# One fused kernel on one core: two tiles turned by TensorE, the last pair's products in another order, and two, not three, second-weight pieces converted in attention

## The chip, the cores and the metric

The kernel runs on one core of a Trainium2 chip. The metric is the device time of one execution in microseconds, as the median of several runs. TensorE multiplies, VectorE (DVE) and ScalarE (ACT) do everything elementwise, GpSimd (POOL) and SyncE (SP) here only issue DMAs.

## What is computed

```python
scores = q @ k.T / sqrt(64) - log(448)           # 4 batches, 12 heads, 448 tokens, 64 wide
x = sigmoid(scores) @ v                          # laid out as 1792 tokens x 768
h = maximum(maximum(x @ w1, x @ w2), x @ w3)     # 768 x 768 each
x = h @ w_out                                    # 768 x 768
h = x @ w_in                                     # 768 x 1024
solu = h * softmax(h)
ln = (solu - mean(solu)) / sqrt(var(solu) + 1e-6) * g_ln
out = ln @ w_out2                                # 1024 x 768
```

Data are float32; the weights arrive as float64 words, which the kernel turns into float32 itself. A matmul runs on numbers split in a high and a low part (hi, lo), as three matmuls: hi by hi, hi by lo, lo by hi.

## The kernel before

**Attention** (span 0 to 203 us) goes over 24 pairs of heads. A visit of a pair has four score products (L253, L257), four sigmoids on ScalarE (L262, L265), and eight matmuls with v (L278) for this pair and the one before. `prep_qk` splits k and q on VectorE, `take_x` copies the result out of PSUM. k, q and v come by SP's queue, v into two buffers in turn. Between pair 12 and the rest, W = w_out @ w_in is formed (`gen_w`, L469), so that later h @ W replaces two layers. Weights come by POOL's queue into five raw buffers (`load_next`, L147); a buffer is loaded again when its weight is done with.

**Background work.** Converting weights is written as generators, and a visit of the second half takes ten steps from them. `convert_w2` converts one piece of w_out2 in 14 steps (two scalings, a multiplication by g, differences, four hi/lo splits on ScalarE and DVE), and SP writes four results to DRAM (L431) through two staging buffers. SECOND says how many of the 16 pieces go beside attention, mixed with the splits of T (12 tiles, two steps each, each one DVE instruction) and the conversion of the first weight group (`convert_group`). LATE says how many go into each of the nine groups of the next stage, RATE how many steps are taken for each matmul there.

**The three 768 x 768 layers** (203 to 434 us): `product` (L604) runs seven products for eight (Strassen-Winograd) in 18 units, with the maximum taken by `sums`. At the end `load_h` fetches h back (hld, L654) and `load_wf` W in two halves of three loads (wf0, wf1; L702). POOL then loads the converted w_out2 from DRAM (w2t, L904).

**Layer 2, SoLU, layer norm and the last layer** (434 us to the end) go over 14 tiles of 128 tokens, in the order 7 to 13, 0 to 6. `layer2` (L682) has 36 matmuls for a tile, into one of two PSUM places; `solu_ln` normalises it on DVE and ScalarE; `split_h` splits the h of the tile after next. Then a tile must be turned. `turn` does it with a DVE transpose of 32 x 32 blocks, a write to DRAM and four reads (L800 to L803); `transposes` with eight transposes on TensorE (L811) and two copies on ScalarE. `plain` names the tiles that take the second way. Two turned tiles are a pair; `operand` splits one of seven operands (A11, A12, S2, S1, S3, S4, A22) into hi and lo with a cast on ScalarE and a subtraction on DVE; `output` runs the seven products P1 to P7 (L864), twelve matmuls each, into four banks x, v, z, w. The names are held in

```python
PROD = {"P1": ("A11", "B11"), "P2": ("A12", "B21"), "P3": ("S4", "B22"), "P4": ("A22", "T4"),
        "P5": ("S1", "T1"), "P6": ("S2", "T2"), "P7": ("S3", "T3")}
```

The first pair's products come after the fourth tile's `layer2`.

**What sets the order.** TensorE's instructions stand in the order of the program everywhere. Up to the end of the three layers that is so for DVE and ScalarE too; in the last part a scheduler orders them, and SP's issues. Each engine, and each queue, goes strictly by its order.

Of the kernel before, what the change touches and what calls it, by code (L numbers as in the profile page):

```python
# [16 lines left out]
P = 128  # L17
# [13 lines left out]
QU, OU = 192, 96  # L31
NG = 3 * FC // 2
RAWS = 5
EARLY, SECOND = 4, 3
LATE = (0, 1, 1, 1, 1, 1, 1, 1, 2)
RING = 10
RATE = (0.46,) + 7 * (0.38,) + (0.4,)
BLOCKS = (3, 0, 1, 2)
WARM = 8
PROD = {"P1": ("A11", "B11"), "P2": ("A12", "B21"), "P3": ("S4", "B22"), "P4": ("A22", "T4"),  # L40
# [5 lines left out]
def sigmoid_attention_max_moe_solu_ln(tc, q, k, v, w123, wo, wi, w2, g, out):  # L46
# [177 lines left out]
    def load_v(pr):  # L224
        if pr >= NP:
            return
        vr = apool.tile([P, 2, 4, D], F32, tag="vr", name=f"vr{pr}", bufs=2)
        sp.dma_start(out=vr, in_=v[pr])
        v_ops[pr] = vr

# [15 lines left out]
    def scores(pr, c):  # L246
        qt, kt = qk_ops[pr]
        sc = ps_sc.tile([P, 2, 512], F32, tag="sc", name=f"sc{pr}_{c}")
        terms = ((0, 0), (1, 0), (0, 1))
        for t, (x, y) in enumerate(terms):  # L250
            start, stop = t == 0, t == len(terms) - 1
            if c == 3:
                pe.matmul(sc[:, 0, :S], lhsT=kt[:, x, c * P :], rhs=qt[:, y], start=start, stop=stop)  # L253
                continue
            for j in range(2):
                rows = slice(j * D, (j + 1) * D)
                pe.matmul(  # L257
                    sc[:, j, :S], lhsT=kt[rows, x, c * P : (c + 1) * P], rhs=qt[rows, y], start=start, stop=stop
                )
        if c == 3:  # L260
            sf = apool.tile([P, S], F32, tag="s3", name=f"sf{pr}_{c}", bufs=2)
            act.activation(sf, sc[:, 0, :S], AF.Sigmoid, bias=bias_s, scale=1.0 / math.sqrt(D))  # L262
        else:
            sf = apool.tile([P, 2, S], F32, tag="sf", name=f"sf{pr}_{c}", bufs=5)
            act.activation(sf, sc[:, :, :S], AF.Sigmoid, bias=bias_s, scale=1.0 / math.sqrt(D))  # L265
        weights[(pr, c)] = sf
# [3 lines left out]
    def attend(pr, n):  # L270
        vr = v_ops[pr]
        c = BLOCKS[n]
        if n == 0:
            pas[pr] = ps_av.tile([P, 512], F32, tag="av", name=f"av{pr}")
        pa = pas[pr]
        sf = weights.pop((pr, c))
        for j in range(2):
            pe.matmul(  # L278
                pa[j * D : (j + 1) * D, :S],
                lhsT=vr[:, j, c],  # L280
                rhs=sf if c == 3 else sf[:, j],
                start=(n == 0),
                stop=(n == 3),
            )
        if n == 3:
            v_ops.pop(pr)
            load_v(pr + 2)

    def take_x(pr):
        pa = pas.pop(pr)[:, :S]  # L290
# [92 lines left out]
    for pr in range(2):  # L383
        load_v(pr)
    prep_qk(0)
    sp.dma_start(out=g_sb, in_=g)
    MID = NP // 2
    for pr in range(MID):
# [49 lines left out]
            return stp.tile([P, 2 * QU], F32, tag="stg", name=name, bufs=2)  # L438
        return state["home"](k, name)

    def mix(first, second, lead=0):
        gens, n = deque([first, second]), 0
        while gens:
            try:
                next(gens[0])
            except StopIteration:
                gens.popleft()
                continue
            yield
            n += 1  # L450
            if n > lead:
                gens.rotate(1)

    pws = {}

# [101 lines left out]
            yield  # L557

    tsplits = [split_t(0, nm, i) for nm in ("T1", "T4", "T3", "T2") for i in range(3)]
    bg.append(mix(run_steps(tsplits + [convert_group(0)]), run_steps(convert_w2(key) for key in w2_second)))  # L560


    attend_rest(MID, 0)
# [91 lines left out]
        hls[t] = hl  # L655

    h2s, lns, uts, lts, hsp = {}, {}, {}, {}, {}
    plain = (tiles[-1],)

    def split_h(t):  # L660
        hh = hsplit.tile([P, FC, P], F32R, tag="hh", name=f"hh{t}")
# [10 lines left out]
                copy(act, hh[:, 4 + f, cols], src)  # L672
                rest(dve, hl[:, 4 + f, cols], src, hh[:, 4 + f, cols])

    def layer2(t, steps):
        if t not in h2s:
            m = tiles.index(t) % 2
            h2s[t] = (ps_h3 if m else ps_h2).tile([P, 2, 512], F32, tag="h2", name=f"h2_{t}")
        hh, hl = hsp[t]
        for n, f in steps:  # L680
            for i, (l, r) in enumerate(((0, 0), (0, 1), (1, 0))):
                pe.matmul(  # L682
                    h2s[t][:, n],
                    lhsT=(hh, hl)[l][:, f],
                    rhs=wfs[f // 3][:, f % 3, r, n * 512 : (n + 1) * 512],
                    start=(f == 0 and i == 0),
                    stop=(f == FC - 1 and i == 2),
                )

    units = [(gi, bp if gi < NG - 1 else 1 - bp) for gi in range(NG) for bp in range(2)]  # L690
    bg.extend(split_t(1, nm, i) for nm, i in FIN)
# [111 lines left out]
            sp.dma_start(out=ut[r * 32 : (r + 1) * 32], in_=u_d[t][:, :, r].rearrange("i f e -> f i e"))  # L803
        uts[t] = ut.rearrange("p i (k t) -> p k i t", k=K2)

    def transposes(t):
        u = lns.pop(t)
        ps = ps_h2.tile([P, 2, 512], F32, tag="h2", name=f"pt{t}").rearrange("p a (k t) -> p (a k) t", k=4)
        ut = tp.tile([P, K2, P], F32, tag="ut", name=f"ut{t}", bufs=3)
        for kc in range(K2):  # L810
            pe.transpose(ps[:, kc], u[:, kc * P : (kc + 1) * P], ident)  # L811
        for n in range(2):
            copy(act, ut[:, 4 * n : 4 * n + 4], ps[:, 4 * n : 4 * n + 4])
        uts[t] = ut.rearrange("p k (i t) -> p k i t", i=4)

    ops, parts = {}, {}

    def part(p, nm):
        t = uts[tiles[2 * p + int(nm[1]) - 1]]
# [14 lines left out]
    def more_operands(p):  # L834
        a11, a12, a21, a22 = (part(p, nm) for nm in ("A11", "A12", "A21", "A22"))
        s1 = tp.tile([P, 4, P], F32, tag="s1", name=f"s1_{p}", bufs=1).rearrange("p k (i t) -> p k i t", i=4)
        tt(s1, a21, a22, ALU.add)
        tt(a21, a11, a21, ALU.subtract)
        tt(a11, s1, a11, ALU.subtract)
        parts.update({(p, "S1"): s1, (p, "S3"): a21, (p, "S2"): a11, (p, "S4"): a12})  # L840
        for nm in ("S2", "S1", "S3"):
            operand(p, nm)
        tt(a12, a12, a11, ALU.subtract)

# [5 lines left out]
        t = f_tile(nm, i, name) if nm != "e" else ew.tile([P, S], F32, tag="e", name=name, bufs=3)  # L850
        return t[:, :HU]

    def output(p, between=None):
        places = "xvzw" if p < TT // 2 - 1 else "zvxw"
        bank = {nm: ps_o.tile([P, 512], F32, tag=at, name=f"o{nm}{p}")[:, :HU] for nm, at in zip("xvzw", places)}

        def prod(b, name, start, stop):
            a, bn = PROD[name]
            op = ops.pop((p, a))
            wt, off, w = next((w2t[n], OU * nms.index(bn), OU * len(nms)) for n, nms in enumerate(PIECES) if bn in nms)  # L860
            for kc in range(4):
                for i, (l, r) in enumerate(((0, 0), (0, 1), (1, 0))):
                    c0 = off + r * w
                    pe.matmul(  # L864
                        bank[b],
                        lhsT=op[:, l, kc],
                        rhs=wt[:, kc, :, c0 : c0 + OU],
                        start=(start and kc == 0 and i == 0),
                        stop=(stop and kc == 3 and i == 2),
                        skip_group_check=True,  # L870
                    )

        def put(i, j, t, cols=slice(0, HU), eng=sp):
            r = tiles[2 * p + i]
            eng.dma_start(out=out[r * P : (r + 1) * P, j * HU : (j + 1) * HU][:, cols], in_=t[:, cols])

        e1, u2, u3, c21 = (block(f"{nm}{p}") for nm in ("e1", "u2", "u3", "cx"))
        prod("x", "P1", True, False)
        act.copy(e1, bank["x"])
        prod("z", "P2", True, True)  # L880
        tt(e1, bank["z"], e1, ALU.add)
        put(0, 0, e1)
        operand(p, "S4")
        operand(p, "A22")
        prod("x", "P6", False, False)
        act.copy(u2, bank["x"])
        prod("v", "P5", True, True)
        tt(u2, bank["v"], u2, ALU.add)
        prod("x", "P7", False, False)
        act.copy(u3, bank["x"])  # L890
        tt(u3, bank["v"], u3, ALU.add)
        put(1, 1, u3)
        prod("w", "P3", True, True)
        tt(u2, bank["w"], u2, ALU.add)
        put(0, 1, u2)
        if between:
            between()
        prod("x", "P4", False, True)
        act.copy(c21, bank["x"])
        put(1, 0, c21)  # L900

    for n in (3, 0, 2, 1):
        for kc in range(4):
            pool.dma_start(out=w2t[n][:, kc].bitcast(F32), in_=w2_d[n][kc])  # L904
    for n, t in enumerate(tiles):
        if n < 2:
            layer2(t, first_f[0 if n else 2 :])
        else:
            layer2(t, [(m, f) for m in range(2) for f in range(FC)])
        solu_ln(t)  # L910
        if t not in plain:
            turn(t)
        if n + 3 < TT:
            load_h(tiles[n + 3])
        if n + 2 < TT:
            split_h(tiles[n + 2])
        if n >= 2 and n % 2 == 0:
            first_operands(n // 2 - 1)
            more_operands(n // 2 - 1)
        elif n >= 3:  # L920
            p = n // 2 - 1
            output(p, (lambda: transposes(tiles[-1])) if n == TT - 1 else None)
    first_operands(TT // 2 - 1)
    more_operands(TT // 2 - 1)
    output(TT // 2 - 1)

    for cm, _ in reversed(p3):
        shut(cm)
# [55 lines left out]
```

## Time and profile before

| what | us |
|---|---|
| three runs: lowest, median, highest | 681.09, 682.87, 684.08 |
| the profiled execution | 678.11 |
| its span, first to last instruction | 676.3 |
| busy: TensorE, DVE, ScalarE | 653.4, 486.6, 316.9 |
| two successive visits of attention begin | 150.68, 156.66 |

The profiled execution is one run of its own, somewhat under the three timed ones; 1.8 us of it lie outside the span. Times in the rows below are counted from the start of the span.

### The profile page before, as it was taken

The page shows a single profiled execution, that of the slowest core. Times are in us where ns is not written, and L with a number is a line of the kernel's source. Part 1 is how long each engine was busy: PE and PEld are TensorE (multiplying, and loading weights), DVE is VectorE, ACT ScalarE, POOL GpSimd, SP SyncE. Part 2 cuts the span into 40 slices and gives each one's busy share as a digit, 9 for nine tenths or more (in the row PEclk, how much of TensorE's full clock was granted, in tenths as well). Part 3 has the DMA queues.
Part 4 walks back from the last instruction along what each step waited for, and adds up shares of the span by engine and source line. Part 5 has one row for each costly group of instructions (what it writes and reads, how often), then busy time and mean ns, then how long its engine had stood idle before and what let it go on. Part 6 is the DMA issues. An engine that isn't in the chain of part 4 may idle for free.

```text
span 676.3 us, 9636 instructions
## 1 busy us (share of the span) xinstructions
PE 653.4 (97%) x3354; PEld 535.4 (79%) x3354; DVE 486.6 (72%) x1052; ACT 316.9 (47%) x639; POOL 53.4 (8%) x103
## 2 busy tenths in 40 slices
PE   9999999999999999999999999995699999999997
PEld 6555588644449999999999999884599898989887
DVE  4799987687768678757777576483849495958573
ACT  5888534688776544444434433231424242324142
POOL 1111111000010110110110100220000000000000
PEclk9999999999999999999999999998799999999999
DMA  8688679955540333531453415999433333233131
GB/s 270 216 259 251 197 243 342 312 162 187 163 162 1 125 110 121 201 119 64 141 175 109 120 64 155 400 404 356 129 100 90 113 104 115 75 98 120 53 110 47
DMA packets 55441, 111.27 MB, mean 165 GB/s; under 512 B 6112, under 2 KB 36832, under 8 KB 54624
## 3 DMA queue, kind: packets, MB, share of 16 engines
q1 hardware_dynamic: 46800, 67.95, 30.7%
q0 software_dynamic: 8448, 42.47, 19.0%
q8 instruction: 26, 0.43, 0.2%
q10 hardware_dynamic: 144, 0.23, 0.1%
q14 instruction: 23, 0.19, 0.1%
HBM read 77.34 MB, written 33.29 MB: 164 GB/s over the span
## 4 chain that ended last, share of the span: by engine, by line
PE 76%; DVE 10%; DMA 7%; ACT 4%; issue 3%; SPq 0%; ACTq 0%; DVEq 0%
PE x L604 19%; PE h L682 13%; PE v L604 10%; PE ox L864 9%; PE av L278 7%; PE z L604 5%; PE sc L257 4%; DMA u_d<-ub 2%; PE ov L864 2%; PE ow L864 2%; PE oz L864 2%; DMA w_d<-ws 2%; PE sc L253 2%; ACT sf L265 1%; DMA ut<-u_d 1%
## 5 line engine op out<-in xcount | busy, mean ns | idle before, releaser
L682 PE MATMUL h<-wf,hh 128*128 128x512 f32 x336 | 103.5, 389 | 0.0
L278 PE MATMUL av<-sf,vr 128*64 128x448 f32 x384 | 77.7, 546 | 0.4 <-DMA vr<-in_v 0.4
L682 PEld LDWEIGHTS h<-wf,hh 128*128 128x128 f32 x336 | 63.0, 188 | 12.8
L265 ACT ACTIVATE sf<-sc,bias_s 128x896 f32<-128x896 f32 x72 | 68.1, 1011 | 2.7 <-PE sc L257 2.4
L682 PE MATMUL h<-wf,hl 128*128 128x512 f32 x168 | 65.4, 389 | 0.0
L278 PEld LDWEIGHTS av<-sf,vr 128*64 128x64 f32 x384 | 25.4, 136 | 41.5 <-issue 35.9
L257 PE MATMUL sc<-qt,kt 64*128 64x448 f32 x432 | 51.7, 376 | 2.3 <-ACT sf L262 2.2
L644 ACT COPY u<-x 128x448 f32<-128x448 f32 x36 | 19.2, 532 | 68.3 <-PE x L604 68.3
L147 POOL DMA_DIRECT2D raw<-in_w x52 | 28.4, 545 | 274.8 <-DVE w2s L57 122.9
L469 PE MATMUL pw<-wi_t,r_wo 128*128 128x512 f32 x216 | 49.6, 390 | 0.0
L257 PEld LDWEIGHTS sc<-qt,kt 64*128 64x128 f32 x432 | 38.5, 184 | 13.6 <-issue 4.8
L469 PEld LDWEIGHTS pw<-wi_t,r_wo 128*128 128x128 f32 x216 | 40.4, 188 | 9.4 <-issue 1.0
L864 PE MATMUL ox<-w2t,opA 128*128 128x384 f32 x168 | 34.5, 355 | 10.4 <-ACT opA L52 10.3
L864 PEld LDWEIGHTS ox<-w2t,opA 128*128 128x128 f32 x168 | 31.2, 198 | 12.1 <-ACT opA L52 11.1
L771 DVE TENSOR_REDUCE st<-h 128x1 f32<-128x1024 f32 x14 | 17.0, 1214 | 32.2 <-PE h L682 32.2
L864 PE MATMUL ox<-w2t,opS 128*128 128x384 f32 x168 | 33.7, 351 | 5.2 <-ACT opS L52 5.2
L682 PEld LDWEIGHTS h<-wf,hl 128*128 128x128 f32 x168 | 31.5, 188 | 6.5
L864 PEld LDWEIGHTS ox<-w2t,opS 128*128 128x128 f32 x168 | 31.1, 196 | 5.8 <-ACT opS L52 5.6
L604 PE MATMUL x<-T3h,S 128*128 128x448 f32 x108 | 33.7, 366 | 0.0
L604 PE MATMUL x<-B11h,A 128*128 128x448 f32 x108 | 33.7, 366 | 0.0
L604 PE MATMUL x<-T2h,S 128*128 128x448 f32 x108 | 33.6, 365 | 0.0
L604 PE MATMUL v<-B22h,S 128*128 128x448 f32 x108 | 33.6, 365 | 0.0
(152 smaller groups left out, 1388.9 us busy)
## 6 DMA issues: line engine op xcount, KB each, us to landing
raw<-in_w POOLq DMA_DIRECT2D x52, 384.0 KB, 3.9
w_d<-w2s SPq DMA_DIRECT2D x48, 192.0 KB, 2.0
w2t<-w_d POOLq DMA_DIRECT2D x12, 768.0 KB, 14.6
u_d<-ub SPq DMA_DIRECT2D x13, 512.0 KB, 3.0
ut<-u_d SPq DMA_DIRECT2D x52, 128.0 KB, 3.1
kr<-in_k SPq DMA_DIRECT2D x24, 256.0 KB, 3.5
vr<-in_v SPq DMA_DIRECT2D x24, 256.0 KB, 3.9
raw<-in_wi POOLq DMA_DIRECT2D x16, 384.0 KB, 4.5
```

The lines of the kernel that those rows point to most:

```text
L147: pool.dma_start(out=t, in_=source(key).rearrange("p (n t) -> p n t", t=2))
L253: pe.matmul(sc[:, 0, :S], lhsT=kt[:, x, c * P :], rhs=qt[:, y], start=start, stop=stop)
L257: pe.matmul(sc[:, j, :S], lhsT=kt[rows, x, c * P : (c + 1) * P], rhs=qt[rows, y], start=start, stop=stop)
L265: act.activation(sf, sc[:, :, :S], AF.Sigmoid, bias=bias_s, scale=1.0 / math.sqrt(D))
L278: pe.matmul(pa[j * D : (j + 1) * D, :S], lhsT=vr[:, j, c], rhs=sf if c == 3 else sf[:, j], start=(n == 0), stop=(n == 3),)
L469: pe.matmul(ps, lhsT=wt[:, a, cols], rhs=wi_t[:, b, c0 : c0 + 512], start=(i == 0), stop=(i == 3 * KC - 1))
L604: pe.matmul(ps, lhsT=l, rhs=r, start=(start and c == 0 and i == 0), stop=(stop and c == 2 and i == 2), skip_group_check=True)
L644: act.copy(e, ps)
L682: pe.matmul(h2s[t][:, n], lhsT=(hh, hl)[l][:, f], rhs=wfs[f // 3][:, f % 3, r, n * 512 : (n + 1) * 512], start=(f == 0 and i == 0), stop=( ...
L771: dve.tensor_reduce(out=nmax, in_=ps, axis=AX.XY, op=ALU.max, negate=True)
L864: pe.matmul(bank[b], lhsT=op[:, l, kc], rhs=wt[:, kc, :, c0 : c0 + OU], start=(start and kc == 0 and i == 0), stop=(stop and kc == 3 and i ...
```

## The change

Four things change. (1) `plain` takes the first two tiles of layer 2 too: they are turned on TensorE, into the four banks of the output products, each behind the first half of the layer of the tile two places on. (2) In the last pair P4 gets a bank of its own and runs third, its operand A22 is split earlier and S3 later, and the operands A11 and A12 are made before the last tile is turned. (3) SECOND is 2 in place of 3, LATE ends with 3 pieces in place of 2, the last RATE is 0.52, and `mix` takes two steps of the first work for one of the second beside attention. (4) v has three buffers, and the sigmoid's small tile one.

```diff
-EARLY, SECOND = 4, 3
-LATE = (0, 1, 1, 1, 1, 1, 1, 1, 2)
+EARLY, SECOND = 4, 2
+LATE = (0, 1, 1, 1, 1, 1, 1, 1, 3)
 RING = 10
-RATE = (0.46,) + 7 * (0.38,) + (0.4,)
+RATE = (0.46,) + 7 * (0.38,) + (0.52,)
...
-        vr = apool.tile([P, 2, 4, D], F32, tag="vr", name=f"vr{pr}", bufs=2)
+        vr = apool.tile([P, 2, 4, D], F32, tag="vr", name=f"vr{pr}", bufs=3)
...
-            sf = apool.tile([P, S], F32, tag="s3", name=f"sf{pr}_{c}", bufs=2)
+            sf = apool.tile([P, S], F32, tag="s3", name=f"sf{pr}_{c}", bufs=1)
...
-            load_v(pr + 2)
+            load_v(pr + 3)
...
     prep_qk(0)
+    load_v(2)
...
-    def mix(first, second, lead=0):
-        gens, n = deque([first, second]), 0
+    def mix(first, second, lead=0, share=1):
+
+        gens, n = [first, second], 0
         while gens:
...
+            at = n >= lead and (n - lead) % (share + 1) == share
             n += 1
-            if n > lead:
-                gens.rotate(1)
+            gen = gens[min(at, len(gens) - 1)]
+            if next(gen, "end") == "end":
+                gens.remove(gen)
+            else:
+                yield
...
-    bg.append(mix(run_steps(tsplits + [convert_group(0)]), run_steps(convert_w2(key) for key in w2_second)))
+    bg.append(mix(run_steps(tsplits + [convert_group(0)]), run_steps(convert_w2(key) for key in w2_second), 0, 2))
...
-    plain = (tiles[-1],)
+    plain = (tiles[0], tiles[1], tiles[-1])
...
+            if (n, f) == (0, FC - 1) and between:
+                between()
...
+        for n, ps in enumerate(banks):
+            for i in range(4):
+                kc = 4 * n + i
+                pe.transpose(ps[:, i * P : (i + 1) * P], u[:, kc * P : (kc + 1) * P], ident)
+        for n, ps in enumerate(banks):
+            copy(act, ut[:, 4 * n : 4 * n + 4], ps.rearrange("p (k t) -> p k t", k=4))
...
+    def turn_first(i):
+        transposes(tiles[i], [ps_o.tile([P, 512], F32, tag="xvzw"[2 * i + m], name=f"pt{i}_{m}") for m in range(2)])
...
-        operand(p, "S4")
-        operand(p, "A22")
+        operand(p, "S3" if p == LAST else "S4")
+        operand(p, "S4" if p == LAST else "A22")
+        if p == LAST:
+            bank["y"] = ps_h3.tile([P, 2, 512], F32, tag="h2", name="oy")[:, 0, :HU]
+            prod("y", "P4", True, True)
         prod("x", "P6", False, False)
...
+        if p == LAST:
+            tt(c21, bank["y"], u3, ALU.add)
+            put(1, 0, c21)
...
+        if p == LAST - 1:
+            first_operands(LAST)
+            turn_last()
         prod("x", "P4", False, True)
...
         else:
-            layer2(t, [(m, f) for m in range(2) for f in range(FC)])
...
+            layer2(t, steps, (lambda: turn_first(n - 2)) if n < 4 else None)
+        if n == 2:
+            finish(1)
+            first_operands(0)
+        elif n == 3:
+            more_operands(0)
+        if n != 1:
+            finish(n)
```

`finish` is `solu_ln` and, for a tile that isn't in `plain`, `turn`.

The first place is ScalarE at the first output pair (tiles 7 and 8; u10 is the exponential of the fourth tile, hh12 the high half of h for the sixth tile, e10 the copy of P1). Before:

```order
L52 CAST opA11_0_4776<-ut7_4607 128x512
L52 CAST opA12_0_4779<-ut7_4607 128x512
L780 ACTIVATE st9_4739<-st9_4739 128x1
L781 ACTIVATE st9_4739<-st9_4739 128x1
L52 CAST hh12_4862<-hld12_4766 128x512
L52 CAST hh12_4862<-hs0_3_2670 128x128
L52 CAST hh12_4862<-hs1_3_2617 128x128
L879 COPY e10_4874<-ox0_4870 128x384
L772 ACTIVATE u10_4836,st10_4833<-h2_10_4796,st10_4833 128x1024
L52 CAST opS2_0_4786<-ut7_4607 128x512
```

and now:

```order
L52 CAST hh12_4874<-hld12_4771 128x512
L52 CAST hh12_4874<-hs0_3_2644 128x128
L52 CAST hh12_4874<-hs1_3_2591 128x128
L774 ACTIVATE u10_4848,st10_4845<-h2_10_4781,st10_4845 128x1024
L890 COPY e10_4886<-ox0_4882 128x384
L52 COPY ut8_4802<-pt1_0_4800 128x512
L52 COPY ut8_4802<-pt1_1_4801 128x512
L52 CAST opS2_0_4835<-ut7_4689 128x512
L52 CAST opS1_0_4838<-s1_0_4831 128x512
L52 CAST opS3_0_4841<-ut8_4802 128x512
```

The casts of A11 and A12 have moved far ahead, in among the work on tile 8. Two copies of the second turned tile (ut8) are new, and stand behind hh12, u10 and e10; the cast of S2 follows them.

The second place is SP's queue at the end of the three layers (w2s are converted pieces on their way to DRAM, hld tiles of h, wf0 and wf1 the halves of W). Before:

```order
L431 DMA w2_d0_99<-w2s3_3_0_4326 128x384
L431 DMA w2_d1_100<-w2s3_3_1_4335 128x384
L431 DMA w2_d2_101<-w2s3_3_2_4344 128x384
L654 DMA hld7_4358<-h_d_103 128x4x128
L654 DMA hld8_4360<-h_d_103 128x4x128
L654 DMA hld9_4362<-h_d_103 128x4x128
L702 DMA wf0_4367<-w_d_98 128x2048 x3
L431 DMA w2_d3_102<-w2s3_3_3_4373 128x192
L702 DMA wf1_4413<-w_d_98 128x2048 x3
```

and now:

```order
L654 DMA hld7_4344<-h_d_103 128x4x128
L654 DMA hld8_4346<-h_d_103 128x4x128
L654 DMA hld9_4348<-h_d_103 128x4x128
L704 DMA wf0_4353<-w_d_98 128x2048 x3
L432 DMA w2_d0_99<-w2s3_3_0_4362 128x384
L432 DMA w2_d1_100<-w2s3_3_1_4370 128x384
L432 DMA w2_d2_101<-w2s3_3_2_4380 128x384
L432 DMA w2_d3_102<-w2s3_3_3_4388 128x192
L704 DMA wf1_4413<-w_d_98 128x2048 x3
```

Three of the four writes of the last piece have moved from ahead of hld7 to between wf0 and wf1.

The third place is TensorE's end, from the transposes of the last tile on (ox, ov, oz, ow, oy are banks, op the operands of pair 5 and, last, 6). Before:

```order
L811 MATMUL pt6_6331<-ident_4420,un6_6233 128x128 x8
L864 MATMUL ox5_6235<-w2t2_4538,opA22_5_6273 128x384 x12
L864 MATMUL ox6_6377<-w2t3_4539,opA11_6_6357 128x384 x12
L864 MATMUL oz6_6379<-w2t0_4536,opA12_6_6360 128x384 x12
L864 MATMUL ox6_6377<-w2t2_4538,opS2_6_6367 128x384 x12
L864 MATMUL ov6_6378<-w2t1_4537,opS1_6_6370 128x384 x12
L864 MATMUL ox6_6377<-w2t1_4537,opS3_6_6373 128x384 x12
L864 MATMUL ow6_6380<-w2t0_4536,opS4_6_6412 128x384 x12
L864 MATMUL ox6_6377<-w2t2_4538,opA22_6_6415 128x384 x12
```

and now:

```order
L814 MATMUL pt_last_6349<-ident_4420,un6_6245 128x128 x8
L875 MATMUL ox5_6247<-w2t2_4538,opA22_5_6285 128x384 x12
L875 MATMUL ox6_6389<-w2t3_4539,opA11_6_6343 128x384 x12
L875 MATMUL oz6_6391<-w2t0_4536,opA12_6_6346 128x384 x12
L875 MATMUL oy_6430<-w2t2_4538,opA22_6_6375 128x384 x12
L875 MATMUL ox6_6389<-w2t2_4538,opS2_6_6382 128x384 x12
L875 MATMUL ov6_6390<-w2t1_4537,opS1_6_6385 128x384 x12
L875 MATMUL ox6_6389<-w2t1_4537,opS3_6_6424 128x384 x12
L875 MATMUL ow6_6392<-w2t0_4536,opS4_6_6427 128x384 x12
```

P4 of the last pair (opA22_6) has moved from the end to the third place, into bank oy.

## Rows read from the trace of the kernel before

**Rows 1.** The page, part 1: busy time of each engine
```profile
PE 653.4 (97%) x3354; PEld 535.4 (79%) x3354; DVE 486.6 (72%) x1052; ACT 316.9 (47%) x639; POOL 53.4 (8%) x103
```

**Rows 2.** Waits on TensorE, whole span: us in total, times, longest
```profile
PE ox L864 <- ACT opA L52: 10.3, 2, 9.2
PE ox L864 <- ACT opS L52: 5.2, 1, 5.2
PE sc L257 <- ACT sf L262: 2.2, 4, 1.0
...
PE av L278 <- DMA vr<-in_v: 0.4, 1, 0.4
```

**Rows 3.** Chain that ended last, 434 to 516 us: start, us, what
```profile
434.15 6.87 PE h L682 x30
...
441.04 1.24 DVE st L771
...
443.54 1.23 DVE u L773
...
449.83 15.94 DMA u_d<-ub
...
467.11 6.83 DMA ut<-u_d
...
474.04 0.63 ACT opA L52
...
485.27 0.60 DVE ut L60
...
485.89 0.63 ACT opS L52
...
486.56 3.78 PE ox L864 x12
490.34 2.16 PE ov L864 x12
...
498.90 16.32 PE h L682 x72
```

**Rows 4.** Stretches: us, busy time of each engine, PEclk, DMA share, GB/s
```profile
140.00:160.00 20.00, 19.59 (x125) 10.24 (x123) 18.23 (x46) 17.20 (x30) 0.76 (x1) 1.00 0.52 168
425.00:430.00 5.00, 5.00 (x26) 4.53 (x25) 1.41 (x5) 2.29 (x6) 0.00 (x0) 1.00 1.02 421
470.00:475.00 5.00, 0.29 (x1) 0.29 (x2) 2.41 (x6) 0.96 (x2) 0.00 (x0) 0.50 0.79 214
485.00:490.00 5.00, 3.44 (x11) 3.22 (x12) 5.00 (x14) 3.11 (x7) 0.00 (x0) 0.66 0.32 92
```

**Rows 5.** Chain that ended last, 640 to 677 us
```profile
653.17 0.89 PE pt L811 x8
...
657.26 0.70 DVE opA L57
...
658.00 2.03 PE ox L864 x10
```

**Rows 6.** ScalarE in order of time, 652 to 658 us
```profile
654.10 1.08 ACT L52 COPY ut<-pt 128x512 f32<-128x512 f32 x2 [2.56 <-PE pt L811]
```

**Rows 7.** Loads of w2t (L904): ns; first and last issue; landing
```profile
L904 POOL DMA_DIRECT2D w2t<-w_d x16: 530/530/562, 434.6 to 454.9; - x16
...
DMA to landing us min/median/max: 5.9/12.5/17.1
```

**Rows 8.** DMA issued 422.82 to 423.5 us: x, KB each, us to landing
```profile
wf<-w_d SPq DMA_DIRECT2D x1, 1024.0 KB, 16.4
```

**Rows 9.** TensorE in order of time, 439 to 440 us
```profile
439.46 0.62 PE L682 MATMUL h<-wf,hh 128*128 128x512 f32 x2
```

**Rows 10.** DMA issued 439 to 443 us
```profile
hld<-h_d SPq DMA_DIRECT2D x1, 256.0 KB, 19.8
```

**Rows 11.** DMA issued 125 to 204 us
```profile
raw<-in_w POOLq DMA_DIRECT2D x8, 384.0 KB, 4.3
```

More of the change, by code (lines that the diff above doesn't have):

```diff
@@ L439, in staging @@
         return state["home"](k, name)
-    def mix(first, second, lead=0):
-        gens, n = deque([first, second]), 0
+    def mix(first, second, lead=0, share=1):
+        gens, n = [first, second], 0
         while gens:
[L444 to L449, printed above, removed]
-            n += 1
-            if n > lead:
-                gens.rotate(1)
+            at = n >= lead and (n - lead) % (share + 1) == share
+            n += 1
+            gen = gens[min(at, len(gens) - 1)]
[3 more added lines that the diff above has]
+                yield
     pws = {}
@@ L673, in split_h, with layer2 @@
                 rest(dve, hl[:, 4 + f, cols], src, hh[:, 4 + f, cols])
-    def layer2(t, steps):
+    def layer2(t, steps, between=None):
         if t not in h2s:
@@ L804, in turn, with transposes, turn_last @@
         uts[t] = ut.rearrange("p i (k t) -> p k i t", k=K2)
-    def transposes(t):
+    def transposes(t, banks):
         u = lns.pop(t)
-        ps = ps_h2.tile([P, 2, 512], F32, tag="h2", name=f"pt{t}").rearrange("p a (k t) -> p (a k) t", k=4)
         ut = tp.tile([P, K2, P], F32, tag="ut", name=f"ut{t}", bufs=3)
[L810 to L813, printed above, removed]
-        uts[t] = ut.rearrange("p k (i t) -> p k i t", i=4)
+        for n, ps in enumerate(banks):
[4 more added lines that the diff above has]
+            copy(act, ut[:, 4 * n : 4 * n + 4], ps.rearrange("p (k t) -> p k t", k=4))
+        uts[t] = ut.rearrange("p k (i t) -> p k i t", i=4)
+    def turn_first(i):
+        transposes(tiles[i], [ps_o.tile([P, 512], F32, tag="xvzw"[2 * i + m], name=f"pt{i}_{m}") for m in range(2)])
+    def turn_last():
+        ps = ps_h2.tile([P, 2, 512], F32, tag="h2", name="pt_last")
+        transposes(tiles[-1], [ps[:, m] for m in range(2)])
     ops, parts = {}, {}
+    LAST = TT // 2 - 1
     def part(p, nm):
@@ L840, in more_operands @@
         parts.update({(p, "S1"): s1, (p, "S3"): a21, (p, "S2"): a11, (p, "S4"): a12})
-        for nm in ("S2", "S1", "S3"):
+        for nm in ("S2", "S1") if p == LAST else ("S2", "S1", "S3"):
             operand(p, nm)
@@ L851, in block, with output @@
         return t[:, :HU]
-    def output(p, between=None):
-        places = "xvzw" if p < TT // 2 - 1 else "zvxw"
+    def output(p):
+        places = "xvzw" if p < LAST else "zvxw"
         bank = {nm: ps_o.tile([P, 512], F32, tag=at, name=f"o{nm}{p}")[:, :HU] for nm, at in zip("xvzw", places)}
@@ L888, in output @@
         tt(u2, bank["v"], u2, ALU.add)
-        prod("x", "P7", False, False)
+        prod("x", "P7", False, p == LAST)
         act.copy(u3, bank["x"])
+        if p == LAST:
+            tt(c21, bank["y"], u3, ALU.add)
+            put(1, 0, c21)
         tt(u3, bank["v"], u3, ALU.add)
@@ L895, in output @@
         put(0, 1, u2)
-        if between:
-            between()
+        if p == LAST:
+            return
+        if p == LAST - 1:
+            first_operands(LAST)
+            turn_last()
         prod("x", "P4", False, True)
@@ L904, in sigmoid_attention_max_moe_solu_ln, with finish @@
             pool.dma_start(out=w2t[n][:, kc].bitcast(F32), in_=w2_d[n][kc])
+    def finish(n):
+        solu_ln(tiles[n])
+        if tiles[n] not in plain:
+            turn(tiles[n])
     for n, t in enumerate(tiles):
+        steps = [(m, f) for m in range(2) for f in range(FC)]
         if n < 2:
@@ L908, in sigmoid_attention_max_moe_solu_ln @@
         else:
-            layer2(t, [(m, f) for m in range(2) for f in range(FC)])
-        solu_ln(t)
-        if t not in plain:
-            turn(t)
+            layer2(t, steps, (lambda: turn_first(n - 2)) if n < 4 else None)
[6 more added lines that the diff above has]
+            finish(n)
         if n + 3 < TT:
@@ L916, in sigmoid_attention_max_moe_solu_ln @@
             split_h(tiles[n + 2])
-        if n >= 2 and n % 2 == 0:
+        if n >= 4 and n % 2 == 0:
             first_operands(n // 2 - 1)
@@ L920, in sigmoid_attention_max_moe_solu_ln @@
         elif n >= 3:
[L921 to L925, printed above, removed]
+            output(n // 2 - 1)
+    operand(LAST, "A22")
+    more_operands(LAST)
+    output(LAST)
     for cm, _ in reversed(p3):
```

## The prediction, made before the changed kernel was run

> **What bounds the kernel now.** I read the page's busy times first: TensorE is busy 653.4 us, 97% of the span [rows 1]. The reader sees there that no other engine is near, and that all that can be won without taking matmuls away is the 23 us in which TensorE stands still, plus what those pauses cost in clock. The waits on TensorE come next [rows 2]: 15.5 us are for operands of the output products (opA, opS), 2.2 us for the sigmoid in attention, 0.4 us for one load of v. The third view, the chain that ended last [rows 3], shows where the 15.5 us lie. The first tile of layer 2 ends at 434.15 + 6.87 = 441.02. A tile takes 16.32 / 2 = 8.16 us (row of 498.90, two tiles), so the four tiles that stand before the first output pair end at 441.02 + 3 x 8.16 = 465.5. The next tile begins at 498.90. Between them lie seven products, which at (498.90 - 490.34) / 4 = 2.14 us each are 15.0 us of work. So 33.4 us pass and 18.4 are lost. The chain names the cause: the write of the first turned tile to DRAM takes 15.94 us and its reading back 6.83, and only at 474.04 does ScalarE cast opA.
>
> Some of the 18.4 us is clock and not waiting. After the wait the granted clock is at 1.2 GHz (0.50) through 470 to 475, and it falls again in the stretch 485 to 490 (0.66) [rows 4]; the product at 486.56 takes 3.78 us instead of 2.14.
>
> **First pair.** Both round trips through DRAM go, with two DVE transposes and ten DMA issues. Added are 16 transposes on TensorE. The trace has eight of them, for the last tile: 0.89 us [rows 5], so 1.8 us for sixteen, all on the path.
>
> The Trainium skill (TensorE: Matmul & The Clock Gate, Part 4: PE-mode transpose) speaks against this: about 275 ns for a transpose in a kernel, and the full clock does not engage for them. By that, an estimate, sixteen take 4.4 us and the time would be 2.6 us longer than by the row. The trace disagrees on the duration (0.11 us each); a fall of the clock after eight of them no row here shows.
>
> Is the first transpose late? Its tile was normalised, turned and on its way to DRAM at 449.83; the transposes stand behind the first half of the third tile, at 441.02 + 8.16 + 4.08 = 453.3. No wait. The second tile is 8.16 us later on both sides, 458.0 against 462.4 with the first 0.9 us in it. No wait either. The operands opA of the first products are ready near 457, so P1 starts straight after the fourth tile, at E = 465.5 + 1.8 = 467.3.
>
> What is late next is opS2, for the third product, P6. In ScalarE's new order the copies of the second turned tile stand behind the cast of h for tile 12 (which waits for the fourth tile to leave its buffer), behind the exponential of the fourth tile, and behind the copy of P1. In the trace the step from a tile's reduction to its product is 443.54 - 441.04 = 2.5 us [rows 3], with the exponential in it. So the product starts at E + 2.5. It takes 1.2; then come two halves of the statistics, s1 and S3, each about as long as the 0.60 of S2 at 485.27, small ones for perhaps 0.2, and S2: it ends at E + 6.9 (S2, its cast and P6 in the old order are the rows of 485.27, 485.89 and 486.56). The cast takes 0.63, and P6 begins at E + 7.6. P1 ends at E + 2.1. P2 must wait, since its bank holds half of the second turned tile: ScalarE is done with the exponential at E + 2.5, copies P1 until E + 2.9, and then the two halves at 0.54 each [rows 6], so P2 runs from E + 3.4 to E + 5.6; this only takes time out of the wait for P6, which is 2.0 us. After two matmuls P6 waits again, for the low half of S2: behind S2 now stand the sum of P2 and S4, about 0.5 and 0.6, then the low half at 0.7 as in [rows 5], so E + 8.8. P6 ends at E + 10.6, four products later it is E + 19.2. The pair takes 1.8 + 19.2 = 21.0 us where it took 33.4: **12.4 us won**. Bounds: 16.6 (18.4 - 1.8) if nothing waits; 10.8 if the clock falls in the new pause, by the 3.78 - 2.14 = 1.6 us that P6 lost before. Each part of the pause is well under the old waits (9.2 and 5.2 [rows 2]), so I take no fall.
>
> Do the products find their weights? The loads of w2t are issued from 434.6 to 454.9 and land at most 17.1 us later, by 472.0 [rows 7]. B11 and B21 are loaded first; the last ones, T1 and T3, are wanted at E + 10.6 = 477.9. Hidden.
>
> **The weights of layer 2 (wf).** A third second-weight piece is now converted in the last group. Its vector work lies under products that keep TensorE busy; if that cover went, its nine DVE instructions, 3.6 us at the mean 18.23 / 46 = 0.40 us of another such stretch [rows 4], would be bare. What isn't free is its place on SP: three writes of 192 KB that went out before the loads of wf now stand between wf0 and wf1. The last load of wf1 is issued at 422.84 and lands 16.4 us later, at 439.2 [rows 8]; the matmul that needs it starts at 439.46 [rows 9]. There is 0.2 us of room. At the 421 GB/s of that time [rows 4] the writes (0.59 MB) take 1.4 us, so TensorE waits 1.2. In the changed program the second and third load of wf1 must also each wait for a landing of wf0; these loads were still queued when wf0 landed, so I add nothing. The upper bound is 2.6: the w2t loads start at 434.6 and can halve what is left of wf1's rate. The lower is 0, since the same writes no longer delay the loads of h ahead of wf0. I take **1.8 us lost**. Behind wf1 in the queue are the loads of h: the one for tile 12 landed by 462.8 [rows 10], and by 2.6 us more it is still ahead of its cast at E.
>
> **The last pair.** P1 waits for its operands now: transposes at 653.17, P4 until 656.2, the low half at 657.26, and ten of P1's matmuls only at 658.00 [rows 5]. In the new order the casts of A11 and A12 stand before P4's copy, but behind them on DVE come s1 and S3 first: turned tile copied at 655.2, two sums of 0.6, low half 0.7, so 657.1 instead of 658.0. P4 moves to a bank of its own and changes no count of products. At the end a DVE sum stands where a ScalarE copy of the same size did. **0.9 us won**, between 0 and 1.4.
>
> **Attention.** The third v buffer takes v2's load out of the path: 0.4 us [rows 2]. The smaller sigmoid buffer costs nothing: its reader comes before the next scores on TensorE. Of the 2.2 us of waits for the sigmoid, with two pieces instead of three the waits on staging writes go. But the fourth block of the first weight group can only be loaded when the first piece has left its raw buffer, takes 4.3 us to land [rows 11], and its scaling now stands on ScalarE ahead of the next sigmoid. Counting the instructions of the new order between the piece's last split and that place I estimate 3.5 us, so ScalarE is held for about 1 us, three scalings stand near, and TensorE waits 1 to 1.8 us. I take **0.4 us won**; bounds -1.0 and 2.2. VectorE: it works 18.23 of 20 us there [rows 4], and two of three background steps are now splits of T instead of one of two. A T step is one DVE instruction, a w2 step 9/14 of one on the mean. A visit of 6 us has ten steps, so 1.7 steps change, worth 1.7 x 5/14 x 0.40 = 0.25 us, or 0.5 if a T instruction is twice the mean: 18.23 / 20 x 6 = 5.5 becomes 5.7 to 6.0, just covered.
>
> **Sum.** 12.4 - 1.8 + 0.9 + 0.4 + 0.4 = 12.3 us. The profiled execution took 678.1 (span 676.3 and 1.8 around it) and would become 665.8. The median of the runs is 682.9, 4.8 above it; the same subtraction gives **670.6**. Runs of before scatter over 3 us, so 0.5%, 3.4 us, is about what can be told from no change.
>
> **Rivals.**
> A, smaller gain: the pause before P6 lets the clock fall (1.6), wf1 costs 2.6 and attention loses 1.0. Gain 12.3 - 1.6 - 0.8 - 1.4 = 8.5, time 674.4. For it: both old waits ended at 1.2 GHz. Against: the new one is shorter.
> B, the transposes are slow, or hold the clock down: 2.6 us, 673.2. For it there is only the page named above; against it 0.11 us in the row.
> C, nothing much changes, because the wait moves to w2t: then T1 and T3 land not by 472 but near 488, time about 680. Against: two tiles' traffic leaves that queue.
> D, slower: VectorE becomes the bound in attention. It decides once a visit costs 1.4 us over its 6 in the nine visits that carry background work, as 9 x 1.4 is all that is won; at 2 us the time is 670.6 + 18 = 688.6. For it: 18.23 of 20. Against: the count of 5.7 to 6.0.
>
> **How the numbers follow.** Forecast 0.66 (its own range 667.5 to 673.5), A 0.20, B 0.04, C 0.05, D 0.05. The lower end takes the forecast without a wf wait (1.8), with the attention waits gone (1.8) and the last pair's bound (0.5): 666.5; the runs of before reach 1.8 below their median and the pause could cost less than I count, so 665. The upper end takes A and the 3 us over which the runs of before scatter: 677.5. Faster by over 0.5%: forecast, A and B, 0.90; same 0.05 (C), slower 0.05 (D).
>
> **What would show it.** Right: TensorE idle about 1.3 us before P2 and 2.0 before P6 of the first pair, clock 1.00 throughout; pair one from the end of the fourth tile in about 19 us; a wait of 1 to 2.5 us in the first tile of layer 2, released by a wf load; P1 of the last pair waiting 0.5 to 0.9. Wrong: transposes over 0.2 us each, clock under 1.00 behind them, opS waiting over 6 us, or visits of attention longer than 6.3 us.

## The result, and the profile after

| | us |
|---|---|
| before: lowest, median, highest of 4 runs | 681.09, 682.69, 684.08 |
| after: lowest, median, highest of 4 runs | 670.60, 673.47, 675.21 |
| ratio after / before, 95% interval | 0.9862, 0.982 to 0.9903 |
| the profiled execution after, and its span | 672.95, 671.2 |

The change wins 9.2 us (1.4%; by the interval 6.6 to 12.3). The forecast was 12.3 us won and 670.6, with a range of 665 to 677.5. The measured 673.5 lies inside it, and the sum of what is won is 3 us too high.

Page of the kernel after, part 1, which answers to [rows 1]:

```profile
PE 657.3 (98%) x3370; PEld 535.0 (80%) x3370; DVE 485.1 (72%) x1051; ACT 318.0 (47%) x642; POOL 53.1 (8%) x103
```

TensorE stands still for 13.9 us now, not 22.9. But its busy time rose by 3.9 us, though only sixteen transposes were added. Keep that for the experiments: it is no doing of the change.

Waits on TensorE in the kernel after, whole span (us in total, times, longest), beside [rows 2]:

```profile
PE h L682 <- DMA wf<-w_d: 3.0, 2, 2.6
PE ox L875 <- ACT opS L52: 1.9, 1, 1.9
PE sc L257 <- ACT sf L262: 1.4, 3, 1.0
PE oz L875 <- ACT ut L52: 1.3, 1, 1.3
...
PE ox L875 <- DVE opA L57: 0.7, 1, 0.7
PE ox L875 <- DVE opS L57: 0.5, 1, 0.5
```

Every wait that was announced is here, and no other of any size is new: for wf, before P2 (oz), before P6 (opS, for its high half cast on ScalarE, then for its low half from DVE), before P1 of the last pair (opA). The wait for v is gone. The chain that ended last shows the same in order of time, beside [rows 3]:

```profile
420.93 10.17 DMA wf<-w_d
431.12 14.29 DMA wf<-w_d
445.46 13.90 PE h L682 x60
459.36 0.87 PE pt L814 x8
460.24 8.21 PE h L682 x36
468.44 0.87 PE pt L814 x8
469.32 4.11 PE h L682 x18
473.45 1.24 DVE st L773
474.71 1.21 ACT u L774 x2
...
481.56 0.61 DVE opS L57
482.22 3.42 PE ox L875 x10
485.64 2.16 PE ov L875 x12
...
494.20 16.32 PE h L682 x72
```

The reader is to see three things. No round trip through DRAM stands in the chain any more. The fourth tile ends at 473.4 and the next tile of layer 2 begins at 494.2, so the pair takes 20.8 us for 15.0 us of work. And ten matmuls of P6 take 3.42 us, where twelve of the next product take 2.16. The windows say why (columns as in [rows 4]):

```profile
440.00:445.00 5.00, 2.45 (x10) 1.39 (x8) 0.00 (x0) 0.00 (x0) 1.51 (x3) 1.00 1.04 398
445.00:450.00 5.00, 4.54 (x20) 3.77 (x21) 2.58 (x5) 2.22 (x5) 1.58 (x3) 1.00 1.02 393
...
468.00:473.00 5.00, 5.00 (x27) 4.22 (x27) 4.25 (x12) 0.41 (x2) 0.00 (x0) 1.00 0.85 315
475.00:480.00 5.00, 2.92 (x15) 2.28 (x14) 4.73 (x12) 2.26 (x5) 0.00 (x0) 1.00 0.65 184
480.00:485.00 5.00, 3.41 (x11) 3.08 (x12) 4.96 (x13) 2.88 (x7) 0.00 (x0) 0.69 0.15 47
```

The granted clock is 1.00 through the second eight transposes (468 to 473) and in the pause behind them, and falls to 1.2 GHz for part of the last row, in which P6 runs.

The view of the waits names ScalarE as what ends the 1.9 us before P6. But ScalarE itself was waiting there:

```profile
476.17 1.08 ACT L52 COPY ut<-pt 128x512 f32<-128x512 f32 x2
480.46 0.62 ACT L52 CAST opS<-ut 128x512 fp32r<-128x512 f32 x1 [3.21 <-DVE ut L60]
```

The second turned tile is copied by 477.25. Then ScalarE stands idle for 3.2 us, because DVE has two halves of the fourth tile's statistics, s1 and S3 ahead of S2, which ends at 480.4. So the wait before P2 is ScalarE's order, and the wait before P6 is ScalarE's order and DVE's together.

### The profile page after: what moved, and what is told of

Read it like the earlier page. It is cut to its first block, busy times and chain, and to the rows that moved or that the text cites. A ratio compares the mean times of both kernels' runs of the same rounds, so it can differ in the third digit from the quotient of the medians.

```text
span 671.2 us, 9648 instructions
## 1 busy us (share of the span) xinstructions
PE 657.3 (98%) x3370; PEld 535.0 (80%) x3370; DVE 485.1 (72%) x1051; ACT 318.0 (47%) x642; POOL 53.1 (8%) x103
## 4 chain that ended last, share of the span: by engine, by line
PE 74%; DVE 9%; issue 9%; DMA 5%; ACT 2%; SPq 0%; POOL 0%; POOLq 0%; DVEq 0%; ACTq 0%
PE x L604 17%; PE h L682 16%; PE v L604 9%; PE ox L875 8%; PE av L278 7%; PE z L604 4%; PE sc L257 4%; DMA wf<-w_d 4%; PE ov L875 2%; PE ow L875 2%; PE oz L875 2%; PE sc L253 2%; DVE y_wo L163 1%; DVE y_wo L159 1%; DVE ws L57 1%
## 5 line engine op out<-in xcount | busy, mean ns | idle before, releaser
L257 PEld LDWEIGHTS sc<-qt,kt 64*128 64x128 f32 x432 | 38.5, 184 | 12.4 <-issue 5.3
L604 PE MATMUL z<-B21h,A 128*128 128x448 f32 x108 | 33.9, 368 | 0.0
L604 PE MATMUL v<-T1h,S 128*128 128x448 f32 x108 | 33.9, 368 | 0.0
L604 PE MATMUL x<-T4h,A 128*128 128x448 f32 x108 | 33.9, 368 | 0.0
```

Source lines behind the costliest of these rows:

```text
L257: pe.matmul(sc[:, j, :S], lhsT=kt[rows, x, c * P : (c + 1) * P], rhs=qt[rows, y], start=start, stop=stop)
L604: pe.matmul(ps, lhsT=l, rhs=r, start=(start and c == 0 and i == 0), stop=(stop and c == 2 and i == 2), skip_group_check=True)
```

## The experiments

Kernels that ran together share their own runs of the kernel before, so ratios are taken against those. Every edit is shown against the changed kernel.

**turns_only**: the kernel before with the two turns on TensorE and nothing else of the change.

```diff
-EARLY, SECOND = 4, 2
-LATE = (0, 1, 1, 1, 1, 1, 1, 1, 3)
-RATE = (0.46,) + 7 * (0.38,) + (0.52,)
+EARLY, SECOND = 4, 3
+LATE = (0, 1, 1, 1, 1, 1, 1, 1, 2)
+RATE = (0.46,) + 7 * (0.38,) + (0.4,)
...
-            load_v(pr + 3)
+            load_v(pr + 2)
```

> Only the two turns on TensorE, everything else as before. Theory (the gain is the first pair's, the wf wait comes from the moved writes): the first pair loses 18.4 us before and 1.8 + 5.8 = 7.6 us in the trace after, so 10.8 us are won and the time is about 671.9. No wait for wf in the first layer-2 tiles, since the writes of the last piece go out ahead of wf0 again. The wait before P6 and its fall of the clock stay (P6's last ten matmuls about 3.4 us). Rival (the wf wait comes from the turns, which start the second and third tile's work in another order): TensorE waits about 3 us for wf here too, 674.9.

670.22 us (median of 4), 683.0 before (13 runs), ratio 0.9823 (0.975 to 0.9895). From the first product of pair 0 to that of pair 1 it is 468.53 to 505.75 = 37.2 us, as after (473.25 to 510.36 = 37.1), and 40.35 before (474.71 to 515.06). The wait of 9.2 us ahead of the first product is gone too. The wf wait is 0.3 us. The theory stands: the turns alone bring the gain, and the wf wait isn't theirs. One expected number was missed: P6's last ten matmuls take 2.62 us here, not 3.4, and the next twelve 3.26 instead of 2.3. The clock fell some 2.2 us behind P6's start instead of 0.8, and stayed low for as long.

**no_turns**: everything but the turns.

```diff
-    plain = (tiles[0], tiles[1], tiles[-1])
+    plain = (tiles[-1],)
...
-            layer2(t, steps, (lambda: turn_first(n - 2)) if n < 4 else None)
+            layer2(t, steps)
```

> Everything but the turns: the second-weight pieces, v buffers and last pair as in the changed kernel, the first two tiles by way of DRAM. Theory (the parts add): attention wins 1.9 us, the last pair 0.7, the wf wait costs 3.0, so the time is 0.4 us above before, 683.1, and a wf wait of about 3 us shows. Rival (the wf wait belongs to the turns): no such wait, 2.6 us won, 680.1.

683.19 us (10 runs), ratio 1.0016 (0.9986 to 1.0047). The wf wait is 2.4 us. The time hit the expected 683.1, but two of its three parts did not come. Attention won nothing here. Nor did the last pair, though its products stand in the new order: its wait is the old 1.1 us. ScalarE in no_turns, then in turns_only, around the last turned tile:

```profile
658.04 1.07 ACT L52 COPY ut<-pt_last 128x512 f32<-128x512 f32 x2 [2.56 <-PE pt_last L814]
660.17 0.48 ACT L919 COPY cx<-ox 128x384 f32<-128x384 f32 x1 [1.05 <-PE ox L875]
660.54 1.66 ACT L52 CAST opA<-ut 128x512 fp32r<-128x512 f32 x3
```

```profile
644.77 1.08 ACT L52 COPY ut<-pt_last 128x512 f32<-128x512 f32 x2 [2.54 <-PE pt_last L813]
645.73 1.15 ACT L52 CAST opA<-ut 128x512 fp32r<-128x512 f32 x2
646.93 0.48 ACT L909 COPY cx<-ox 128x384 f32<-128x384 f32 x1
```

In turns_only the casts go ahead of the copy of P4 (cx), in no_turns behind it, though only no_turns has the products in the new order. What decided the 0.7 us was which way the scheduler laid these rows. Between these two kernels that came with the turns; in by_hand below, which has both the turns and the new order of products, the rows are laid the old way again.

**old_pieces**: the changed kernel with the second-weight pieces distributed as before (the same lines as in turns_only, v buffers kept). **sooner**: two pieces stay beside attention as in the change, but the last group has two instead of three, and the group before it two.

```diff
-LATE = (0, 1, 1, 1, 1, 1, 1, 1, 3)
-RATE = (0.46,) + 7 * (0.38,) + (0.52,)
+LATE = (0, 1, 1, 1, 1, 1, 1, 2, 2)
+RATE = (0.46,) + 6 * (0.38,) + (0.5, 0.4)
...
-                bg.append(mix(late, convert_group(u[0] + 1), 4) if u[0] + 1 < NG else late)
+                bg.append(mix(late, convert_group(u[0] + 1), 18 if n == 14 else 4) if u[0] + 1 < NG else late)
```

> The changed kernel with the second-weight pieces distributed as before (3 beside attention, 2 in the last group, rate 0.4, shares 1 to 1). Theory: the wf wait (3.0 us) goes, and of attention's 1.9 us about 1.5 go with it, since only the v wait (0.4) belongs to the v buffers; 673.5 - 3.0 + 1.5 = 672.0. Rival (attention's gain comes from the third v buffer): only the wf wait goes, 670.5. If the wf wait stays, 675.0.

> The changed kernel with one of the last group's three second-weight pieces moved into the group before it, so that the last group has two pieces and its old rate: attention as in the changed kernel, the last writes ahead of wf0 as before. Theory (the three writes between wf0 and wf1 make the wf wait): the wait of 3.0 us goes and attention's gain stays, 670.5. Rival (wf1 is late because TensorE reaches it sooner, or from the traffic of the h loads): the wait stays at 2 us or more, 673. In all four runs of this call a second question: a product matmul of the three layers began every 203 ns on the mean in the trace of before and every 207 ns in that of after. If that belongs to the kernel's edits, the runs differ by their edits; if it belongs to the single execution, both values turn up without regard to them, and 4.5 us of span go with it.

670.78 us (ratio 0.9831, 0.9778 to 0.9883) and 670.01 (0.9812, 0.9756 to 0.9868). In sooner no wait for wf is left; in old_pieces 1.5 us. The theory for old_pieces, that attention would give back 1.5 us (672.0), was not borne out; its rival's 670.5 is nearer. So the place of the last writes matters, but the wait scatters from execution to execution: with the writes ahead of wf0 it is 0 (before), 0.3, 0, 1.5, and 1.3, 0.9, 0, 0 in the runs below, 0.5 on the mean of eight; with the writes between wf0 and wf1 it is 3.0 (after), 2.4 (no_turns), and 2.4, 3.1 below, 2.7 on the mean of four. The change costs 2.2 us there. The times alone don't tell sooner from old_pieces.

**before_again** and **after_again** are the two kernels unchanged.

> The kernel before, unchanged, for the pace of the product matmuls (203 ns in before, turns_only and no_turns, 207 ns in after, old_pieces and sooner). If the pace belongs to the program, it is 203 ns here and the ratio is 1.000. If it belongs to the execution, it may be 207, and then the span is about 4.5 us above the 676.3 of the first trace; the times of one kernel then fall into two groups 4 to 5 us apart.

> The changed kernel, unchanged. If the pace of the product matmuls belongs to the program, it is 207 ns again; if to the execution, 203 ns may show, with a span about 4.5 us under the 671.2 of the first trace. The second half of attention took 71.0 us in the first trace and 72.2 in no_turns, which has the same code there: if that is scatter, it is anything between 70.9 and 72.5 here, and the wf wait of 3.0 us can vary by about 1.

682.83 us (10 runs, ratio 1.0023, 0.9989 to 1.0057) and 671.02 (4 runs, ratio 0.9867, 0.9825 to 0.9909). One window of before, after, before_again and after_again, in this order:

```profile
210.00:420.00 210.00, 210.00 (x1037) 194.44 (x1036) 150.21 (x329) 91.51 (x210) 19.50 (x36) 1.00 0.36 118
```

```profile
210.00:420.00 210.00, 210.00 (x1018) 190.75 (x1017) 148.97 (x328) 91.57 (x211) 20.04 (x37) 1.00 0.37 117
```

```profile
210.00:420.00 210.00, 210.00 (x1018) 190.64 (x1017) 148.35 (x325) 89.73 (x207) 19.55 (x36) 1.00 0.35 113
```

```profile
210.00:420.00 210.00, 210.00 (x1037) 194.44 (x1036) 152.09 (x338) 93.24 (x216) 20.04 (x37) 1.00 0.37 121
```

In the same 210 us, at the same full clock and without a pause, TensorE does 1037 product matmuls or 1018: one every 202.8 ns or every 206.7. The pace changes sides when a kernel is run again, so it belongs to the execution and not to the edits; both paces turn up among the kernels that ran together. From the first to the last of the 1134 matmuls of the stage it makes 4.1 to 4.4 us (231.2 against 235.3 to 235.6). It is the rise in TensorE's busy time seen above (after_again has 653.5 us), and probably the greater part of the 4.8 us by which the first trace of before lies under its median; the timed runs have no trace that would show it. At the pace of 203 ns the spans are 676.3 before and 668.2 after, at 207 ns 682.2 and 671.2: 8.1 and 11.0 us apart, 9.6 on the mean, where the two first traces give 5.1.

The repeats settle attention too. From the first score of the second half to its end it takes 79.7, 80.1, 78.6 and 79.4 us in the four traces with the old distribution (before, turns_only, old_pieces, before_again), and 78.4 to 80.1, mean 79.3, in the eight with the new one. The pieces won nothing that shows. One wait was exchanged for others, by the mechanism that the prediction named: in the four traces with the old distribution TensorE waits behind two staging writes, 1.2 to 2.3 us together; in the eight with the new one these waits are gone, but ScalarE waits 0.95 to 2.09 us for the load of a raw buffer (L155), and TensorE 0.99 to 2.16 us behind it. In sum TensorE's waits for the sigmoid come to 2.0 us on the mean of either group. The third v buffer won a little: the first half takes 122.9 us on the mean of the three traces with two buffers, and 122.4 on that of the nine with three. The two groups overlap (122.5 to 123.4 and 122.2 to 122.8), but the wait for v, 0.4, 1.0 and 0 in the three, is in none of the nine.

**by_hand**: the changed kernel, with ScalarE's and DVE's order around the first pair written out, so that ScalarE no longer stops at the cast of h for tile 12 before it copies the second turned tile. **by_hand_sooner** has the edit of sooner as well.

```diff
+            if n == 3:
+                by_hand = pin(ET.Activation, ET.DVE)
             layer2(t, steps, (lambda: turn_first(n - 2)) if n < 4 else None)
...
             more_operands(0)
+            output(0, lambda: (finish(3), load_h(tiles[6]), split_h(tiles[5])))
+            shut(by_hand)
+            continue
...
         prod("v", "P5", True, True)
+        if between:
+            between()
```

> The changed kernel, with the order on ScalarE and DVE written out by hand around the first pair: the copies of the second turned tile and the casts of S2, S1, S3 stand before the cast of h for tile 12, and the exponential of the fourth tile behind the copy of P6. Theory (the pause before P2 and P6 is ScalarE's order, and the pause makes the clock fall): the waits of 1.3, 1.9 and 0.5 us go and so do the 1.6 us of slower clock, 5.3 us in all, 668.2; from the first product of pair 0 to that of pair 1 it is 31.9 us instead of 37.1, and the granted clock stays at 1.00. Rival 1 (the transposes bring the clock down, not the pause): the waits go, P6 still takes over 3 us, 669.8. Rival 2 (DVE holds S2 back, since it normalises the third tile until 473.2): a wait of about 1 us stays before P6, 669.3.

> The order by hand and the second-weight piece moved out of the last group together. Theory (the two pauses are independent): 5.3 + 3.0 us less than the changed kernel, 665.2, with neither the wf wait nor a fall of the clock in the first pair. Rival (with wf on time the loads of w2t are what the first pair waits for): a wait on w2t of 1 to 3 us in the first pair, 667.

670.25 us (ratio 0.9849, 0.98 to 0.9898) and 666.84 (0.9797, 0.9758 to 0.9837), beside after_again's 671.02. The expected 668.2 and 665.2 were missed by 2.1 and 1.6 us. The rival of by_hand_sooner, a wait for w2t, did not show either. TensorE in by_hand, first pair:

```profile
473.70 2.28 PE L875 MATMUL ox<-w2t,opA 128*128 128x384 f32 x12
475.82 2.29 PE L875 MATMUL oz<-w2t,opA 128*128 128x384 f32 x12
477.94 2.32 PE L875 MATMUL ox<-w2t,opS 128*128 128x384 f32 x12
480.10 2.32 PE L875 MATMUL ov<-w2t,opS 128*128 128x384 f32 x12
482.26 2.29 PE L875 MATMUL ox<-w2t,opS 128*128 128x384 f32 x12
484.38 2.31 PE L875 MATMUL ow<-w2t,opS 128*128 128x384 f32 x12
488.71 3.92 PE L875 MATMUL ox<-w2t,opA 128*128 128x384 f32 x12 [2.01 <-ACT u L906]
```

Six products now run without a pause. So the waits before P2 and P6 were the order on ScalarE and DVE, and the transposes don't slow what follows them. Both orders were written out at once, so how much of the wait before P6 each of them made is not shown. But my order put the copy of P7's result (u L906) behind the fourth tile's norm, and P4, which adds to the same bank, waits 2.0 us for it. Behind that pause the clock falls again (3.92 us for twelve matmuls). The pause had moved, not gone; none of the rivals said so. The last pair's 1.1 us wait also came back.

**no_pause**: by_hand_sooner with that copy ahead of the norm's last steps. **no_pause_last**: also the last pair's casts by hand.

```diff
-    def solu_ln(t):
+    def solu_steps(t):
...
+        yield
         act.activation(s0, z, AF.Ln)
...
         act.copy(u3, bank["x"])
+        if between:
+            next(between, None)
...
+            at_end = pin(ET.Activation, ET.DVE)
             first_operands(LAST)
             turn_last()
```

> by_hand_sooner with one more change of order: ScalarE copies the result of P7 before the two small steps of the fourth tile's norm and before the cast of h for tile 12, where by_hand_sooner has it behind them. Theory (a late copy of the bank x stalled P4 for 2.8 us and the clock fell behind that pause): no wait in the first pair, clock 1.00 through it, 31.4 to 31.9 us from the first product of pair 0 to that of pair 1 instead of 35.9, and 4.4 us less than by_hand_sooner, 662.5. Rival (the fourth tile's turn is now too late for the second pair): the wait turns up at the first S operand of pair 1, and the first two pairs together win less than 2 us.

> no_pause with the casts of A11 and A12 of the last pair placed by hand ahead of the copies of the last turned tile. Theory (P1 of the last pair waits 0.7 us only because the scheduler puts these casts behind the copies): the wait before the last pair's P1 goes, 17.3 us from the transposes' end to the last matmul instead of 18.0, 0.7 us less than no_pause. Rival (the turned tile itself lands late, since it comes through DRAM): the wait stays.

665.01 us (6 runs, ratio 0.9751, 0.9713 to 0.9789) and 663.32 (6 runs, 0.9715, 0.9671 to 0.9759). All the waits of TensorE in no_pause_last:

```profile
PE sc L257 <- ACT sf L262: 1.8, 3, 1.4
PE pwarm L381 <- DVE warm L97: 1.1, 1, 1.1
```

In no_pause it is 470.14 to 501.41 from the first product of pair 0 to that of pair 1, 31.3 us, as between the later pairs; in both the clock is 1.00 until the last matmul, and no wait for wf is left. From the start of the last pair's last transpose to that of its last matmul it takes 17.0 us, against 18.0 in no_pause. The median of no_pause is 2.5 us above the 662.5 expected; its trace is one of the pace of 207 ns. no_pause_last has the lowest median here, though the 1.7 us between it and no_pause lie within the scatter of the runs: against its own runs of before it wins 18.8 us (by the interval 16.4 to 22.4), twice what the change won.

## Why the prediction was right, and where its sum was off

**First pair: right in mechanism and in its steps, 1.4 us too much.** The working had P6 begin at E + 7.6 and go on at E + 8.8, with E the end of the fourth tile: 480.9 and 482.1 from E = 473.25. The trace has 481.13 and 482.22. The pause before P2 was to be 1.3 and is 1.3. The transposes were to take 1.8 us and take 0.87 each eight in the chain, 1.6 in all as TensorE's starts tell it. The failing step is "Each part of the pause is well under the old waits (9.2 and 5.2 [rows 2]), so I take no fall": the clock fell behind 1.9 and 0.5 us with two matmuls between, and P6's ten matmuls took 3.42 where 1.8 were due. That was the lower bound named there (10.8). The pair wins 18.4 - 1.6 - 5.8 = 11.0, not 12.4.

**wf: right in cause, with a term put at nothing.** The step's 1.8 was taken between the 1.2 of the writes alone and the bound of 2.6. The profiled run waited 3.0, and 2.7 against 0.5 on the mean makes 2.2. The writes were sized rightly: from the landing of the last load of wf0 to that of the first of wf1 it takes 4.2 us on the mean of the four traces with the writes between, 2.9 on that of the eight without, so 1.3 where 1.4 was reckoned. The failing step is "these loads were still queued when wf0 landed, so I add nothing". In those four traces the last load of wf1 is issued just as a load of wf0 has landed (431.12 in the chain above, where the load issued at 420.93 took 10.17), and it lands 4.0 to 4.3 us behind the load before it; in the eight it is issued ahead and lands 2.6 to 3.5 behind, 3.0 on the mean. That is some 1.2 us more. Whether the late issue slows it or the w2t loads beside it was not tried. "0.2 us of room" was also less firm than it looked: with the old order of writes the wait came to 1.3 and 1.5 in two traces.

**Last pair: 0.7 measured, 0.9 predicted, the reason only half right.** That the casts stand ahead of P4's copy was the right row. It is not an effect of the reordered products: no_turns has them and wins nothing, turns_only lacks them and wins 0.7.

**v and attention.** The v buffer wins 0.5 us on the mean (0.4 predicted); the moved piece 0.1 (0.4 predicted), less than the executions scatter. The wait for the raw buffer came as foreseen (1 to 1.8 predicted, 1.0 to 2.2 in the eight traces), but it costs as much as the waits that it replaced. VectorE did not become the bound, so rival D falls. The sign "visits longer than 6.3 us" could not tell: behind its first visit the second half has four of them before (6.4 to 7.3 us) and two after (6.4 and 7.3).

**Sum.** 11.0 - 2.2 + 0.7 + 0.5 + 0.1 = 10.1, measured 9.2 with 6.6 to 12.3 around it. Of the rivals A came nearest, and its 674.4 is nearer to the measured 673.5 than the forecast's 670.6: its clock loss and its late wf1 both happened, its loss in attention did not. Rival B's page, the Trainium skill (TensorE: Matmul & The Clock Gate, Part 4: PE-mode transpose), gives 275 ns for a transpose and no full clock. The trace's record of each transpose is 272 ns long, but they start 0.11 us apart, and eight took 0.87 us; so the prediction's "the trace disagrees on the duration" holds for the pace and not for one transpose. The clock was 1.00 in the stretch that holds them.

The step "the same subtraction" held, but by way of medians alone. Had only one trace been taken of each kernel, the pace would have hidden nearly half of the gain.

## What to carry to other kernels

Count in a predicted pause the clock behind it as well as the wait: the cure is to take the pause away, which shortened the first pair by 5.8 us more (37.1 to 31.3). When a wait is removed by another order on an engine, follow every later reader of the same bank or buffer, since the wait goes to whatever was put last. And before two traces are compared, compare how many equal matmuls they do in a stage that the edits don't touch.

## What the runs showed that was not expected

- Two paces of the same matmuls at the same granted clock of 1.00: 448 columns every 202.8 ns in five traces (before, turns_only, no_turns, by_hand_sooner, after_again) and every 206.7 in the other seven. What chooses between them stays open.
- A pause does not always bring the clock down: the wf wait of 2.6 us in the kernel after, near 443, was followed by a clock of 1.00, while 1.9 us before P6 and 2.0 us before P4 (by_hand) were followed by some 3.4 us at 1.2 GHz. What separates the two wasn't tried.
- An edit in one place reorders another: the two turns at 460 us changed the scheduler's order of three rows at 650 us, worth 0.7 us, and the order by hand of the first pair changed it back.
